# Decay attention and a squared-ReLU layer pair on one core: visits spaced apart, one product moved into a shared bank, and every engine's order planned anew

## The chip, the core and the metric

The kernel runs on one core of a Trainium2 chip, as one launch. The metric is the device time of that launch in microseconds (us), from three runs of the same program. One execution was also recorded by the hardware profiler. The engines are named as in the profile: PE (TensorE, the matrix engine; PEld are its weight loads), DVE (VectorE), ACT (ScalarE), POOL (GpSimd) and SP (SyncE, which here only issues transfers).

## The reference

```python
def _attn_ref(q, k, v, lam):                 # B=4, H=8, S=768, D=64, blocks of 64
    ...
    Dmask = np.where(rel >= 0, lam[:, None, None] ** rel[None, :, :], 0.0)
    ...
    for b in range(nb):
        ...
        intra = np.einsum('bhij,bhjd->bhid', np.einsum('bhic,bhjc->bhij', qb, kb) * Dmask[None], vb)
        inter = np.einsum('bhid,bhde->bhie', qb * lam_pow[None], kv_state)
        out[:, :, sl] = intra + inter
        kv_state = lam_block[...] * kv_state + np.einsum('bhsd,bhse->bhde', kb * rev_pow[None], vb)

def _moe_ref(x, w_in, w_out):                # x: 3072 tokens x 512, w_in: 512 x 2048, w_out: 2048 x 512
    h = np.maximum(x @ w_in, 0.0)
    return (h * h @ w_out).astype(np.float32)
```

The attention's output, with its heads side by side, is the input x of the two layers. Everything is 32-bit floating point, and the kernel keeps nearly that accuracy: each operand of a large product is split into a rounded part ("hi") and a remainder ("lo"), and three of the four partial products are summed.

## The kernel before, in words

**Chunks.** The 3072 tokens are 24 chunks of 128 tokens. Chunks 0 to 3 are the first of each batch; they are computed whole at the front, one after the other (scores of the chunk, sums for its state, its result). The other 20 go in pairs, in *visits*: one visit finishes the old pair (its results, in two halves: state products, `bank<-s,qv` and `bank<-qv,hold` in the trace) and opens the new one (its scores, `bank<-qv,ka`). All are small multiplications (64x64). The table `VISITS` says before which step a visit's first and second part stand: the result halves in one, the rest in the other. Between them the values of a chunk have to be scaled by powers of the decay, either by eight ScalarE multiplications of 128x64 (L564) or by one VectorE multiplication of 128x512 (L567); `weighted` chooses by the chunk's number. `dot` copies (L736) on ScalarE tie the two halves of a result together: PE's next half waits for them.

**Layers.** Four chunks make a tile of 512 tokens. For tiles 0 and 1 the first layer is 32 *steps* (`first_layer`, L770), one for each tile and each block of 128 hidden columns, of 12 multiplications 128x512; the results go through ReLU and square on ScalarE (L781, L782), and those not kept go to one of two buffers `sp` and from there to memory (spilled, L785). For the very first two blocks a step is cut in halves of 256 columns, so that the first half can go ahead of chunks 2 and 3. The other 16 chunks go in two passes (p = 0, 1) of four tiles as a scheme of seven products for a 2x2 block multiplication: `first_products` makes 8 groups of 7 products (each six multiplications 128x512, 1.36 us), `second_products` makes 56 products for the second layer. Within a group, products 1, 6 and 7 accumulate in bank "x", 2 in "y", 5 and 3 in "v", 4 in "z"; ScalarE copies the running sum of "x" to buffers `u` (r1, r2, r3; L893), so that product 6 waits for copy r1 and 7 for r2; VectorE adds bank and copy (L897), and ScalarE applies ReLU and square (L898, L899). The passes stand in this order: steps with visits; first products of p = 0; second products of p = 0; second products of tiles 0 and 1 (called p = 2), with five more visits between them (`INSIDE`); first and second products of p = 1.

**Weights.** Differences of weight blocks are made by VectorE (L820 to L826), split by ScalarE and VectorE (L804, L805), written to memory (`kept<-pw`) and read back by each product (`b<-kept`, L862) into few buffers `b`: four for the first 16 reads. A second-layer product takes its hidden block from ScalarE's cast and VectorE's remainder (L943, L944), which are let go three products ahead.

**Order.** No engine's order stands in the source. Each operation is entered with its dependences, its buffers and a modelled cost; `Plan.order` then sets the order of each engine by modelled time and a number for each operation, the long table `DUE`. The program is written out in that order, so each engine works its own list strictly in turn, and SP's list is the order in which all transfers are issued. The constants `FETCH`, `FETCH_LATER` and `FETCH_END` are the planner's cost of a refill of PE's program code, and up to which modelled time which of them holds. The code itself comes by a queue of its own, "q8 instruction" in the profile.

## Time and profile before

| | us |
|---|---|
| time, median of 3 runs (lowest, highest) | 557.48 (554.11, 558.42) |
| the profiled execution's own time | 559.53 |
| its span, first to last instruction | 557.8 |
| PE busy | 542.3 (97%) |
| DVE busy | 448.5 (80%) |
| ACT busy | 355.4 (64%) |
| mean busy share of the 16 DMA engines, whole span | about 0.8 |
| mean granted clock of TensorE | 0.993 of full |

PE is at work nearly all the time. So the table is read from its rest: 557.8 less 542.3 leaves 15.5 us without a matrix multiplication, and a mean clock below 1 says that some of the busy time ran slow. Where both lie is what the waits and the timeline of PE tell.

### The profile page before, as it was taken

The page shows a single profiled execution, that of the slowest core. Times are in us where ns is not written, and L with a number is a line of the kernel's source. Part 1 is how long each engine was busy: PE and PEld are TensorE (multiplying, and loading weights), DVE is VectorE, ACT ScalarE, POOL GpSimd, SP SyncE. Part 2 cuts the span into 40 slices and gives each one's busy share as a digit, 9 for nine tenths or more (in the row PEclk, how much of TensorE's full clock was granted, in tenths as well). Part 3 has the DMA queues.
Part 4 walks back from the last instruction along what each step waited for, and adds up shares of the span by engine and source line. Part 5 has one row for each costly group of instructions (what it writes and reads, how often), then busy time and mean ns, then how long its engine had stood idle before and what let it go on. Part 6 is the DMA issues. An engine that isn't in the chain of part 4 may idle for free.

```text
span 557.8 us, 12919 instructions
## 1 busy us (share of the span) xinstructions
PE 542.3 (97%) x4822; PEld 446.6 (80%) x4822; DVE 448.5 (80%) x897; ACT 355.4 (64%) x758; POOL 5.1 (1%) x10
## 2 busy tenths in 40 slices
PE   8898999998999999889999999999999999999997
PEld 7786787886888888768888888888888888888885
DVE  4999798998999999969967779999923334579864
ACT  4699677885799989844544333456456667655441
POOL 3000000000000000000000000000000000000000
PEclk9999899998999999999999999999999999999999
DMA  8978799989999867889999999447876776777763
GB/s 300 333 257 307 259 331 316 334 273 345 337 330 349 317 227 264 274 302 317 342 335 337 352 335 315 136 132 191 240 255 195 194 193 194 195 189 214 210 184 113
DMA packets 73406, 148.19 MB, mean 266 GB/s; under 512 B 7936, under 2 KB 14848, under 8 KB 73344
## 3 DMA queue, kind: packets, MB, share of 16 engines
q1 hardware_dynamic: 73056, 147.22, 80.2%
q8 instruction: 38, 0.62, 0.4%
q14 instruction: 24, 0.20, 0.1%
q10 hardware_dynamic: 288, 0.14, 0.1%
HBM read 106.18 MB, written 41.16 MB: 264 GB/s over the span
## 4 chain that ended last, share of the span: by engine, by line
PE 55%; DVE 6%; DMA 3%; issue 1%; ACT 0%; DVEq 0%; SPq 0%
PE bank L517 55%; DMA b<-kept 2%; DVE h L897 2%; DVE v L944 1%; DVE pw L805 1%; DVE part L805 1%; DMA kept<-part 0%; DVE m L494 0%; DVE m L826 0%; DMA kept<-pw 0%; DVE rs L826 0%; DVE m L496 0%; DVE h L951 0%; DVE m L492 0%; DVE rs L820 0%
## 5 line engine op out<-in xcount | busy, mean ns | idle before, releaser
L517 PE MATMUL bank<-v,b 128*128 128x512 f32 x1008 | 232.9, 391 | 3.1 <-ACT pw L804 1.5
L517 PEld LDWEIGHTS bank<-v,b 128*128 128x128 f32 x1008 | 188.1, 188 | 44.3 <-issue 3.0
L943 ACT CAST v<-h 128x512 fp32r<-128x512 f32 x168 | 101.8, 622 | 100.4 <-PE bank L517 73.4
L944 DVE TENSOR_TENSOR v<-h,v 128x512 fp32r<-128x512 f32 x168 | 113.5, 689 | 33.5 <-ACT v L943 29.8
L770 PE MATMUL bank<-xs,wi 128*128 128x512 f32 (+1 forms) x408 | 94.6, 388 | 4.3 <-issue 2.2
L770 PEld LDWEIGHTS bank<-xs,wi 128*128 128x128 f32 x408 | 74.2, 192 | 20.1 <-issue 2.5
L897 DVE TENSOR_TENSOR h<-bank,u 128x512 f32<-128x512 f32 x64 | 43.9, 691 | 46.1 <-ACT u L893 32.1
L951 DVE TENSOR_TENSOR h<-h,h 128x512 f32<-128x512 f32 x96 | 63.7, 689 | 0.8 <-DMA h<-spill 0.3
L898 ACT ACTIVATE h<-h 128x512 f32<-128x512 f32 x64 | 39.8, 628 | 13.4 <-DVE h L897 12.9
L899 ACT ACTIVATE h<-h 128x512 f32<-128x512 f32 x64 | 39.9, 630 | 0.7
L893 ACT COPY u<-bank 128x512 f32<-128x512 f32 x48 | 27.8, 580 | 14.9 <-PE bank L517 14.5
L564 ACT ACTIVATE qv<-qv,small 128x64 f32<-128x64 f32 x123 | 32.0, 339 | 3.8 <-POOL small L438 3.5
L517 PE MATMUL bank<-qv,ka 64*64 64x64 f32 (+2 forms) x1344 | 31.2, 224 | 0.7 <-issue 0.3
L517 PEld LDWEIGHTS bank<-qv,ka 64*64 64x64 f32 (+2 forms) x1344 | 27.8, 139 | 3.7 <-issue 2.2
L804 ACT CAST pw<-m 128x256 fp32r<-128x256 f32 x56 | 21.5, 403 | 9.3 <-DVE m L826 4.9
L805 DVE TENSOR_TENSOR pw<-m,pw 128x256 fp32r<-128x256 f32 x56 | 22.9, 423 | 3.2 <-ACT pw L804 3.0
L517 PE MATMUL bank<-sum_s,b 128*128 128x512 f32 x96 | 24.5, 391 | 0.0
L490 ACT ACTIVATE m<-st 128x512 f32<-128x512 f32 x32 | 21.2, 675 | 4.7 <-DMA st<-w 4.7
L517 PE MATMUL bank<-sum_a,b 128*128 128x512 f32 x96 | 24.2, 389 | 0.0
L517 PE MATMUL bank<-sum_a,wi 128*128 128x512 f32 x96 | 24.2, 389 | 0.0
L517 PEld LDWEIGHTS bank<-s,qv 64*64 64x64 f32 (+1 forms) x704 | 16.0, 137 | 9.2 <-issue 4.6
L517 PE MATMUL bank<-sum_t,part 128*128 128x512 f32 x96 | 23.1, 389 | 0.0
(83 smaller groups left out, 632.4 us busy)
## 6 DMA issues: line engine op xcount, KB each, us to landing
b<-kept SPq DMA_DIRECT2D x224, 256.0 KB, 3.1
st<-w SPq DMA_DIRECT2D x32, 512.0 KB, 4.9
kept<-pw SPq DMA_DIRECT2D x56, 256.0 KB, 3.6
ka<-ka SPq DMA_DIRECT2D x23, 512.0 KB, 5.8
qv<-qv SPq DMA_DIRECT2D x23, 512.0 KB, 6.1
kept<-part SPq DMA_DIRECT2D x32, 256.0 KB, 3.0
kept<-wi SPq DMA_DIRECT2D x24, 256.0 KB, 3.8
out<-end SPq DMA_DIRECT2D x23, 256.0 KB, 3.6
```

The costliest lines, as they stand in the source:

```text
L517: nc.tensor.matmul(*args, **kw, skip_group_check=True)
L564: self.o_vd = [plan.op("ACT", act(D) + 0.11, key, lambda i=i: nc.scalar.mul(v()[:, i], v()[:, i], wdec[:, i:i + 1]), [self.o_qv[1], o_pow] ...
L770: nc.tensor.matmul(at(h)[:, cs], wt[:, cc, :], xt[:, cc, cs], start=k == 0, stop=k == 3 * NCC - 1)
L804: oh = plan.op("ACT", act(256), key, lambda: nc.scalar.copy(at(part)[:, 0], side(k)), deps, raws + [part])
L805: ol = plan.op("DVE", tt(256), key, lambda: nc.vector.tensor_tensor(out=at(part)[:, 1], in0=side(k), in1=at(part)[:, 0], op=ALU.subtract), ...
L893: return plan.op("ACT", act(WIDE) - 0.03, key - 6, lambda: nc.scalar.copy(at(dst), at(banks[k])), [o], [banks[k], dst])
L897: o = plan.op("DVE", tt(WIDE), key - 6, lambda: nc.vector.tensor_tensor(out=at(b), in0=at(banks[k]), in1=at(a), op=ALU.add), deps, [banks[ ...
L898: o1 = plan.op("ACT", act(WIDE) + 0.01, key, lambda: nc.scalar.activation(at(b), at(b), AF.Relu), [o], [b])
L899: o1 = plan.op("ACT", act(WIDE) + 0.01, key, lambda: nc.scalar.activation(at(b), at(b), AF.Square), [o1], [b])
L943: oh = plan.op("ACT", act(WIDE) + 0.01, key - 16, lambda: nc.scalar.copy(rounded[hi.slot], at(b)), made[t, 2 * j + e], [b, hi], after)
L944: ol = plan.op("DVE", tt(WIDE), key - 16, lambda: nc.vector.tensor_tensor(out=rounded[lo.slot], in0=at(b), in1=rounded[hi.slot], op=ALU.su ...
L951: made[o] = [plan.op("DVE", tt(WIDE), when, lambda: nc.vector.tensor_tensor(out=at(h[o]), in0=at(h[a]), in1=at(h[b]), op=op), deps + made[ ...
```

## The change: spacing, a bank, a split and a new plan

What it does:

- `VISITS` moves the second part of the sixth visit from step 23 to step 25, and the last visit from step 27 to step 28. `INSIDE` moves three second parts by one or two products.
- `VS_END = 24`: the values of chunks 16 to 23 are scaled by eight ScalarE multiplications each instead of one VectorE multiplication.
- In `first_products` bank "z" is gone. Product 4 accumulates onto bank "x" after 1, 6 and 7, and waits for copy r3; its block is then ReLU straight from the bank (`squared` holds the square), so that one VectorE addition per group (16 in all) vanishes. Product 1 of the next group moves between 7 and 4.
- `FETCH`, `FETCH_LATER`, `FETCH_END` change, and `DUE` is all new; with it every engine's order. The DUE rows below stand for the whole table.

```diff
 DUE = [
-    0, 1, 2, 3, 2, 14, 5, 6, 5, 6, 8, 13, 18, 17, 7, 15, 9, 12, 14, 18, 29, 24, 13, 37, 32, 33, 36, 37, 41, 40, 16, 46, 43, 44, 46, 47, 54, 48, 10,
+    0, 1, 2, 3, 2, 18, 6, 17, 1, 0, 11, 17, 14, 20, 10, 28, 23, 8, 16, 31, 43, 35, 13, 35, 19, 12, 29, 34, 38, 41, 14, 46, 40, 21, 42, 39, 57, 49, 16,
...
-FETCH, FETCH_LATER, FETCH_END = 4.5, 3.2, 40.0
+FETCH, FETCH_LATER, FETCH_END = 4.75, 3.3, 260.0
...
-HALVED, HALF_KEY = 2, 3.0
+HALVED, HALF_KEY, VS_END = 2, 3.0, 24
...
-VISITS = [(3, 3), (6, 7), (10, 11), (14, 15), (18, 19), (22, 23), (27, 27)]
-INSIDE = [(1, 4, 4), (1, 11, 14), (1, 19, 22), (1, 27, 30), (1, 36, 36)]
+VISITS = [(3, 3), (6, 7), (10, 11), (14, 15), (18, 19), (22, 25), (28, 28)]
+INSIDE = [(2, 4, 4), (2, 11, 16), (2, 19, 23), (2, 26, 30), (2, 36, 36)]
 FIRST_ORDER = [1, 2, 6, 5, 7, 4, 3]
-AT_ONCE = [1, 2, 4, 6, 5, 7, 3]
+AT_ONCE = [1, 2, 6, 5, 7, 4, 3]
...
-            split = (VS if self.i else VS_FIRST) if self.i < N_ALONE else VS_LATER if self.i < N_PLAIN + 8 else 0
+            split = (VS if self.i else VS_FIRST) if self.i < N_ALONE else VS_LATER if self.i < VS_END else 0
...
-        banks, r, h, made = {k: Buf("bank") for k in "xyvz"}, [Buf("u" if p or j else "u0") for _ in range(3)], hidden[p], ready_h[p]
-        where = {1: "x", 2: "y", 6: "x", 5: "v", 7: "x", 4: "z", 3: "v"}
+        banks, r, h, made = {k: Buf("bank") for k in "xyv"}, [Buf("u" if p or j else "u0") for _ in range(3)], hidden[p], ready_h[p]
+        where = {1: "x", 2: "y", 6: "x", 5: "v", 7: "x", 4: "x", 3: "v"}
...
-                x, first = sums[g][:, :, k:k + 2], i in (1, 2, 5, 4)
+                x, first = sums[g][:, :, k:k + 2], i in (1, 2, 5)
...
+        def squared(t, f, o):
+            b = h[t, f]
+            made[t, f] = [plan.op("ACT", act(WIDE) + 0.01, key, lambda: nc.scalar.activation(at(b), at(b), AF.Square), [o], [b])]
...
             if i == 4:
-                st["p4"] = product(4)
-            if "r3" in st and "p4" in st:
-                block("z", 1, f0, r[2], [st.pop("p4"), st["r3"]])
+                b, o = h[1, f0], product(4, [st["r3"]])
+                squared(1, f0, plan.op("ACT", act(WIDE) - 0.02, key - 6, lambda: nc.scalar.activation(at(b), at(banks["x"]), AF.Relu), [o], [banks["x"], b]))
...
             k = order.index((j, 1))
-            order[k - 1], order[k] = order[k], order[k - 1]
+            order.insert(k - 2, order.pop(k))
...
-            if (j, i) == order[-1]:
+            if (j, i) == order[-2]:
                 product(LAST_ORDER[0], 0, twice[p])
```

Lines after the table stand one or two higher in the new program (L517 is L518 there, L781 is L782).

PE at the end of the front, before: chunk 3's sums (`64x64 x8`), its result (`bank<-s,qv`, eight rows of which the first two are shown), and then the second halves of the steps of blocks 0 and 1. `wi_66` and `wi_67` are the weights of those blocks.

```order
L517 MATMUL bank_65<-qv_3_89,ka_3_85 128x128
L770 MATMUL bank_59<-xs_220,wi_67 128x256 x12
L517 MATMUL bank_60<-qv_3_89,ka_3_85 64x64 x8
L517 MATMUL bank_58<-s_3_133,qv_3_89 64x128
L517 MATMUL bank_58<-s_2_132,qv_3_89 64x128
...
L770 MATMUL bank_61<-xs_220,wi_66 128x256 x12
L770 MATMUL bank_59<-xs_220,wi_67 128x256 x12
L770 MATMUL bank_62<-xs_220,wi_68 128x512 x12
```

The same place in the changed program (`table` rows are filler multiplications, whose result nobody reads):

```order
L518 MATMUL bank_65<-qv_3_89,ka_3_85 128x128
...
L518 MATMUL bank_59<-qv_3_89,ka_3_85 64x64 x8
L443 MATMUL bank_63<-table_219 128x128
L518 MATMUL bank_63<-s_3_133,qv_3_89 64x128
L518 MATMUL bank_63<-s_2_132,qv_3_89 64x128
...
L771 MATMUL bank_60<-xs_220,wi_67 128x256 x12
L771 MATMUL bank_61<-xs_220,wi_66 128x256 x12
L771 MATMUL bank_60<-xs_220,wi_67 128x256 x12
L771 MATMUL bank_58<-xs_220,wi_68 128x512 x12
```

The first half of block 1's step (`wi_67`) moved from ahead of chunk 3's sums to behind its result.

ACT around the last visit's `dot` copies, before: `sp` blocks are ReLU and square of a step, `pw` casts belong to weight differences, `m<-st` begins the conversion of a loaded weight block, `sum_a<-xk` belongs to the new pair's operands.

```order
L781 ACTIVATE sp_168<-bank_62 128x512
L782 ACTIVATE sp_168<-sp_168 128x512
L804 CAST pw_190<-m_162 128x256
L781 ACTIVATE sp_167<-bank_61 128x512
L736 COPY small<-bank_60 128x1
L490 ACTIVATE m_162<-st_206 128x512
L736 COPY small<-bank_63 128x1
L782 ACTIVATE sp_167<-sp_167 128x512
```

The same place in the changed program:

```order
L782 ACTIVATE sp_167<-bank_63 128x512
L805 CAST pw_190<-m_164 128x256
L783 ACTIVATE sp_167<-sp_167 128x512
L491 ACTIVATE m_162<-st_206 128x512
L491 ACTIVATE m_164<-st_205 128x512
L782 ACTIVATE sp_168<-bank_62 128x512
L737 COPY small<-bank_60 128x1
L783 ACTIVATE sp_168<-sp_168 128x512
L737 COPY small<-bank_64 128x1
```

A step's ReLU still stands directly ahead of the copies; the conversions of two weight blocks moved ahead of it, and no `pw` cast is left between the two.

PE in the first groups of pass 0, before (one row is one product; products 1, 2, 6, 5, 7, 4 of group 0 with 1 of group 1 behind 4, then 3; `sum_` names the token operand):

```order
L517 MATMUL bank_60<-sum_a,wi_66 128x512 x6
L517 MATMUL bank_59<-sum_a,wi_66 128x512 x6
L517 MATMUL bank_60<-sum_s,part_187 128x512 x6
L517 MATMUL bank_63<-sum_t,part_185 128x512 x6
L517 MATMUL bank_60<-sum_t,part_186 128x512 x6
L517 MATMUL bank_58<-sum_z,part_188 128x512 x6
L517 MATMUL bank_64<-sum_a,wi_68 128x512 x6
L517 MATMUL bank_63<-sum_s,wi_67 128x512 x6
```

The same place in the changed program:

```order
L518 MATMUL bank_59<-sum_a,wi_66 128x512 x6
L518 MATMUL bank_64<-sum_a,wi_66 128x512 x6
L518 MATMUL bank_59<-sum_s,part_187 128x512 x6
L518 MATMUL bank_61<-sum_t,part_185 128x512 x6
L518 MATMUL bank_59<-sum_t,part_186 128x512 x6
L518 MATMUL bank_58<-sum_a,wi_68 128x512 x6
L518 MATMUL bank_59<-sum_z,part_188 128x512 x6
L518 MATMUL bank_61<-sum_s,wi_67 128x512 x6
```

Product 4 (`sum_z`) now writes the bank of 1, 6 and 7, and one product stands between it and 7.

## Rows read from the trace of the kernel before

**Rows 1.** The page: PE's busy time, and PE's code queue (packets, MB, share).

```profile
PE 542.3 (97%) x4822; PEld 446.6 (80%) x4822; DVE 448.5 (80%) x897; ACT 355.4 (64%) x758; POOL 5.1 (1%) x10
...
q8 instruction: 38, 0.62, 0.4%
```

**Rows 2.** Waits of PE: line, releaser, us in total, times, longest.

```profile
PE bank L770 <- issue: 2.2, 1, 2.2
PE bank L517 <- ACT small L736: 2.1, 1, 2.1
PE bank L770 <- ACT xs L632: 1.9, 1, 1.9
PE bank L517 <- ACT pw L804: 1.5, 1, 1.5
...
PE bank L517 <- DMA b<-kept: 1.0, 2, 0.7
PE bank L517 <- ACT v L943: 0.5, 1, 0.5
PE bank L517 <- issue: 0.3, 1, 0.3
PE bank L517 <- ACT qv L564: 0.3, 1, 0.3
```

**Rows 3.** Stretches: length, busy PE, PEld, DVE, ACT, POOL, clock, DMA share, GB/s.

```profile
55.20:58.70 3.50, 3.50 (x10) 2.74 (x9) 3.50 (x10) 0.82 (x2) 0.00 (x0) 0.51 0.97 335
...
133.70:137.20 3.50, 3.50 (x68) 3.02 (x65) 3.24 (x10) 2.81 (x8) 0.00 (x0) 0.51 0.98 312
50.00:52.41 2.41, 2.40 (x129) 2.01 (x128) 2.14 (x5) 2.37 (x6) 0.00 (x0) 1.00 1.03 394
```

**Rows 4.** PE's timeline at the front's end: start, length, group, idle before.

```profile
23.20 1.68 PE L770 MATMUL bank<-xs,wi 128*128 128x256 f32 x12
```

**Rows 5.** VectorE's timeline in the same stretch.

```profile
26.88 0.69 DVE L700 TENSOR_TENSOR xr<-bank,rdec 128x512 f32<-128x512 f32 x1
```

**Rows 6.** PE's timeline around the visit before the eighth step.

```profile
51.90 0.51 PE L770 MATMUL bank<-xs,wi 128*128 128x512 f32 x1
54.62 7.58 PE L770 MATMUL bank<-xs,wi 128*128 128x512 f32 x25 [2.21 <-issue]
```

**Rows 7.** ScalarE at the last visit of the first part.

```profile
132.74 0.60 ACT L781 ACTIVATE sp<-bank 128x512 f32<-128x512 f32 x1 [0.26 <-DMA spill<-sp]
133.24 0.15 ACT L736 COPY small<-bank 128x1 f32<-128x1 f32 x1
```

**Rows 8.** Stretches of the same view as rows 3: first products, then later ones.

```profile
140.00:194.00 54.00, 54.00 (x240) 44.71 (x239) 53.05 (x123) 47.92 (x105) 0.00 (x0) 1.00 0.97 338
194.00:234.00 40.00, 39.25 (x174) 32.14 (x172) 40.00 (x90) 37.05 (x78) 0.00 (x0) 1.00 0.70 239
234.00:256.00 22.00, 19.67 (x82) 15.07 (x83) 16.70 (x30) 10.20 (x18) 0.00 (x0) 1.00 0.93 319
256.00:400.00 144.00, 144.00 (x1549) 119.37 (x1548) 128.15 (x237) 67.95 (x127) 0.00 (x0) 1.00 0.83 275
```

**Rows 9.** Groups by line: busy us, mean ns, idle before and releasers.

```profile
L897 DVE TENSOR_TENSOR h<-bank,u 128x512 f32<-128x512 f32 x64 | 43.9, 691 | 46.1 <-ACT u L893 32.1 <-PE bank L517 13.3
...
L564 ACT ACTIVATE qv<-qv,small 128x64 f32<-128x64 f32 x123 | 32.0, 339 | 3.8 <-POOL small L438 3.5 <-DMA qv<-qv 0.2
L893 ACT COPY u<-bank 128x512 f32<-128x512 f32 x48 | 27.8, 580 | 14.9 <-PE bank L517 14.5
...
L567 DVE TENSOR_TENSOR qv<-qv,small 128x512 f32<-128x512 f32 x8 | 5.5, 687 | 0.0
```

**Rows 10.** Transfers of the page: KB each, median us from issue to landing.

```profile
qv<-qv SPq DMA_DIRECT2D x23, 512.0 KB, 6.1
```

**Rows 11.** The page's groups of casts and remainders for second-layer products.

```profile
L943 ACT CAST v<-h 128x512 fp32r<-128x512 f32 x168 | 101.8, 622 | 100.4 <-PE bank L517 73.4
L944 DVE TENSOR_TENSOR v<-h,v 128x512 fp32r<-128x512 f32 x168 | 113.5, 689 | 33.5 <-ACT v L943 29.8
```

More of the change, by code (lines that the diff above doesn't have):

```diff
@@ L1039 @@
     twice = [first + 56 * A_PROD]
-    twice = [twice[0], 0, twice[0] + 56 * A_PROD]
+    twice = [twice[0], 0, twice[0] + 56 * A_PROD + STRETCH * 2 * sum(not p for p, _, _ in INSIDE)]
     third = twice[2] + 56 * A_PROD + STRETCH * 8
@@ L1049, in visit_at @@
         p, a, c = INSIDE[v - len(VISITS)]
-        return twice[2] + A_PROD * a + STRETCH * sum(x <= a for _, x, _ in INSIDE) * 2
+        return twice[p] + A_PROD * a + STRETCH * 2 * sum(x <= a and q == p for q, x, _ in INSIDE)
     chunks = []
@@ L1116, in firsts @@
             k = order.index((j, 1))
-            order[k - 1], order[k] = order[k], order[k - 1]
+            order.insert(k - 2, order.pop(k))
         for j, i in order:
-            if (j, i) == order[-1]:
+            if (j, i) == order[-2]:
                 product(LAST_ORDER[0], 0, twice[p])
             runs[j](i)
-            if j == NF // 2 - 1 and i in (2, 6, 3):
+            if j == NF // 2 - 1 and i in (2, 7, 4):
                 gate[p].append(end[0])
@@ L1128, in seconds @@
             for j in range(NF // 2):
-                for v, (_, a, c) in enumerate(INSIDE):
-                    if p == 2 and n == a:
+                for v, (q, a, c) in enumerate(INSIDE):
+                    if (p, n) == (q, a):
                         one, two = visiting(len(VISITS) + v)
@@ L1134, in seconds @@
                             rest[c] = two
-                if p == 2 and n in rest:
+                if p != 1 and n in rest:
                     linked(rest.pop(n))
```

4 lines of the change are left out of this document (1 added, 3 removed), and 167 rows, old and new, of the table DUE.

## The prediction, as it stood before the run

> **What bounds the kernel now.** I read the page first, for which engine is at work all the time: PE, with 542.3 us of the span, while the rest idle far more [rows 1]. Then PE's waits, because 15.5 us is all that PE leaves, and they come in a few pieces [rows 2]: one wait for "issue" (2.2, called B here), one for the dot copies of L736 (2.1, C), one for the cast L632 (1.9, A), and three behind one another in the second products of pass 0 (1.5, 1.0 for two, 0.5: together 3.0, D). Two of 0.3 follow; the start and the end hold most of the rest and are not touched by the change. Then the granted clock by stretches: right after B and right after C it is 0.51, for about 3.5 us each [rows 3], that is the lower of the two levels (1.2 instead of 2.4 GHz). Each costs 3.5 × 0.49 = 1.7 us more. After the waits of 1.9 and 1.5 no stretch shows it. So the most that a better order can return is A 1.9, B 2.2 + 1.7, C 2.1 + 1.7, D 3.0 and 0.6: 13.2 us. Elsewhere PE runs through: 54 of 54 us and 144 of 144 [rows 8], at 1.36 us a product. The number of products is the same after the change, so work that other engines are spared counts only where it ends one of these waits.
>
> **The sum by parts.** The profiled execution took 559.53 us; I make the sum against that, and then go to the median of the three runs, 557.48, which is 2.05 lower.
>
> *A, end of the front.* Chunk 3's result has to go through an addition on VectorE (L700, 0.69) and a cast on ScalarE before the step of block 0 can go on, and the addition began at 26.88, behind other work of a VectorE that has no gap there [rows 5]. PE waits 1.9. The new order puts the first half of block 1's step, which needs only chunks 0 and 1, into that place; such a half takes 1.68 us [rows 4]. In its old place between two pieces of chunk 3 it would be missed only if chunk 3's scores then hold PE up, and there the new plan has filler and half of block 0's step. Cover alone returns 1.68. VectorE has also less between the last operands, since conversions of weight blocks stand later. I take the whole wait, 1.9. Bounds: 0.3, if the wait reappears ahead of chunk 3's result for want of that half; 2.8, if the chunk's loads, which the new order of transfers puts ahead of one 512 KB weight load each, also pull the chain forward by some 0.9.
>
> *B, the wait for issue.* PE's program came in 38 blocks of 0.62 MB together; 4822 multiplications and 4822 loads in 38 blocks are 254 instructions each [rows 1]. A first-layer step needs 24 instructions for 2.72 us, so that a block lasts some 29 us; but the visit before the eighth step has 129 multiplications and 128 loads, a whole block, in 2.41 us, with the DMA engines full [rows 3]. PE stops one multiplication of the step further, for 2.2 us [rows 6]: I read this as the next block still on its way. The new plan leaves out one filler multiplication and, counting the instructions of both programs, the block ends four rows later, after two more multiplications of that step, 0.2 us each. If the block arrives when it did, the wait is 2.2 − 0.45 = 1.75. That is between the 1.5 and 1.9 that left the clock at full and away from the 2.1 and 2.2 that didn't, so I take it that the slow stretch goes too: 0.45 + 1.7 = 2.1. Bounds: −0.3 (block a little later, clock falls) and 3.9 (all of it).
>
> The Trainium skill speaks against this term: "Runtime: NRT & Kernel Launch", section "Instruction fetch mechanics", says that code is prefetched in order and that crossing a 16 KiB boundary costs little, mostly hidden. The row of 2.2 us differs at one crossing of 38, and agrees for nearly all others. By that rule B would have another cause, its term would be 0, and the sum below 2.1 smaller (the second rival).
>
> *Small waits.* The 0.3 for issue has the same cause, in the visit at step 23; its second part now stands at 25, two steps of 2.72 us more between the parts. The 0.3 for L564 is a visit's scaling that comes late. Both go: 0.6, bounds 0 and 0.6.
>
> *C, the last visit.* ScalarE does its list in order. Just ahead of the dot copy at 133.24 stands the ReLU of a step, which waits for a spill of one of the two `sp` buffers and ends its 0.60 us only then [rows 7]; PE waits for the copy, 2.1. In the new order a step's ReLU still stands directly ahead, but the visit stands one step later in the program and the step before it is not the one that has just handed over a buffer, and no `pw` cast stands between. I reckon with 1.0 left, which is the copy's own way plus the one ReLU that PE cannot avoid (0.60 [rows 7]) and its wait, and with no fall of the clock: 1.1 + 1.7 = 2.8. Bounds: −0.5 (same wait with a weight block's conversion, which waits for its load, in the list ahead) and 3.8.
>
> *D, the reads of weight differences.* PE waits here for operands of which the last to come are reads `b<-kept` [rows 2], in a stretch with the DMA engines at 0.93 [rows 8]. The transfers of that stretch are the same in kind and number in the new list. VectorE is better off: it is busy 40.00 of 40.00 us up to 234 [rows 8], and eight additions fewer in pass 0 are 8 × 691 ns = 5.5 us [rows 9]. But what PE waits for last is the transfer, and SP issues it when a buffer comes free, not when VectorE is done. Term 0; bounds −1.5 and 2.5, the latter if stores of differences leave earlier and clear the queue.
>
> *Product 4 in the shared bank.* 16 additions on VectorE go (8 × 0.69 a pass). In exchange product 4 waits for copy r3. One product, 1.36 us, now stands between 7 and 4; the copy takes 0.58 [rows 9], so it has 0.7 us to spare. Before, the same copies r1 and r2 stood under 6 and 7 in the same way, and PE lost nothing by them from 140 to 194 [rows 8]. The copies themselves mostly wait for PE (14.5 us idle before them, 48 of them [rows 9]), so ScalarE is there in time, except where it is full (37 of 40 us from 194 to 234 [rows 8]). If a copy comes 0.9 late there, product 4 loses 0.2. Term −0.4; bounds 0 and −1.0. Pass 1's groups are free: PE is all that is busy there.
>
> *Values on ScalarE.* Eight VectorE multiplications (5.5 us) become 64 of 339 ns each (21.7 us) [rows 9]. ScalarE has 68 of 144 us in the stretch where they fall [rows 8], and no addition or cast waits there that isn't covered by the three products that casts run ahead, so 0. What it costs without that cover is the third rival.
>
> *Give-back.* From 140 to 194 the DMA engines are at 0.97 and VectorE at 53 of 54 [rows 8]. If PE arrives there 6 us earlier, less slack is left, and a part may come back as waits of products for differences or for hidden blocks. VectorE's own saving by then is about that of the additions passed so far. I take −1.0; bounds 0 and −3.
>
> Sum: 1.9 + 2.1 + 0.6 + 2.8 + 0 − 0.4 + 0 − 1.0 = 6.0. Profiled execution: 559.5 − 6.0 = 553.5; on the median's scale 557.5 − 6.0 = **551.5 us**.
>
> **Rivals.**
>
> 1. *D goes as well.* If VectorE's 5.5 us bring the stores forward, the reads at 230 to 251 find a freer queue: up to 2.5 more, and with B and A at their upper bounds some 2 more. For it: the stretch before it moves only 0.70 of what the DMA engines can [rows 8], so there is room for earlier stores. Against: SP's list is in order. Time: about 548 (546 to 549.5).
>
> 2. *The clock still falls, or B is not what I take it for.* If both remaining waits are followed by a slow stretch, 3.4 comes back: 555. If B stays whole, 2.1 comes back, 553.6; with a give-back of 3, as PE runs into a VectorE and a DMA that are full from 140 on, 556 to 557. For it: the two waits differ by only some tenths from those with a clock fall. The change then does little that can be measured.
>
> 3. *Slower: ScalarE held by a late chunk.* The 64 new multiplications stand in ScalarE's list, and the first of each eight waits for its chunk, 512 KB, 6.1 us median from issue to landing [rows 10]. Before, VectorE took that wait. Behind them in the list stand the casts for coming second-layer products. A cast may begin three products ahead, 4.08 us; cast and remainder take 0.62 + 0.69 [rows 11], so some 2.7 us are to spare. It decides from where the load lands more than 2.7 us after ScalarE has reached the multiplication. Each of the eight chunks then stops PE for the excess; eight times 1.5 us is 12, which ends the gain and makes 551.5 + 12 = 563.5. With a wait of more than 2 us, the clock might fall too. Against it: the new list puts three to four products and visit parts between issue and multiplication, about the load's median, so a wait of 0 to 2 us is likelier, which is covered.
>
> **How the numbers follow.** A measurement of this kernel can tell about 1% from no change, 5.6 us, so 551.9 and 563.1 are the marks. Forecast (550 to 553.5) 0.40, a little over half of it below 551.9; rival 1 0.24; rival 2 and the give-back (553.5 to 559) 0.25; rival 3, or another new wait of its size, 0.11. Faster by over 1%: 0.23 + 0.24 = 0.47. Slower by over 1%: of the last case, and a little for costs that nobody priced, 0.11. Within 1%: 0.42. The range leaves out the lower end of rival 1 and rival 3: 546 to 558.5; its upper end is the sum with the bounds of B, C and the give-back taken together (−0.3, 0.5, −3 instead of 2.1, 2.8, −1: 558).
>
> **What would show it.** A: no wait of L771's matmuls for L633, and block 0's second half beginning before 28. B: the wait for issue between 1.4 and 2.0 us, clock 1.00 in the stretch behind it. C: the wait for L737 about 1, clock full behind it. Small: no wait in the visit at step 23 or 25. D: waits of about 3 us for `b<-kept` at the same products. Product 4: L898 (before L897) 48 times instead of 64, PE whole from 140 to 194. Values: L565 187 times instead of 123, and no wait of PE for L944 in 256 to 400. What would make it wrong: waits of PE of over a microsecond where there are none now, above all in the second products of p = 2, or a new long wait for issue, since the code's blocks end elsewhere in all later visits.

## The result, and the profile after

The changed kernel takes 551.58 us (median of 11 runs, 550.62 to 553.66), the kernel before on the same chip 557.79 (11 runs, 553.69 to 559.69): a ratio of 0.9905, with an interval of 0.9878 to 0.9931. That is 6.2 us less; 6.0 were forecast. The profiled execution took 553.66 us with a span of 551.9, 5.9 less than before, and is the longest of the eleven, as the profiled one of before was near its longest. So the two can be set beside each other, and the question is whether the 5.9 are made of the terms that were forecast. They are only partly, and the profiled execution is not the usual one.

The page's first line of engines, to be read against [rows 1]:

```profile
PE 540.5 (98%) x4820; PEld 446.2 (81%) x4820; DVE 434.6 (79%) x873; ACT 370.2 (67%) x822; POOL 5.1 (1%) x10
```

VectorE has 24 instructions and 14 us less, ScalarE 64 instructions and 15 us more, as the two edits say. The waits of PE after, to be read against [rows 2]:

```profile
PE bank L518 <- DMA b<-kept: 2.6, 2, 2.0
PE bank L518 <- ACT small L737: 2.1, 1, 2.1
PE bank L443 <- DVE table L427: 1.5, 1, 1.5
PE bank L771 <- DVE xs L634: 0.7, 1, 0.7
PE bank L771 <- issue: 0.4, 1, 0.4
PE bank L518 <- issue: 0.2, 1, 0.2
```

A has gone from 1.9 to 0.7, B from 2.2 to 0.4, both small waits are gone and one of 0.2 is new, at another visit (81 us); C is what it was, 2.1, and D is 2.6 instead of 3.0. What each stretch gained is read best from windows cut at the same instruction in both kernels, so that each holds the same work (the counts of PE are the same but for missing records). The cuts are the first multiplications of the third first-layer step (the first whole one) and of the ninth, the first product of pass 0, the 57th and the 78th, and PE's last. Before:

```profile
31.64:58.84 27.20, 24.98 (x459) 20.32 (x458) 26.85 (x61) 21.79 (x56) 0.00 (x0) 0.94 0.86 295
58.84:150.09 91.25, 88.49 (x1409) 72.98 (x1408) 81.39 (x194) 69.20 (x183) 0.00 (x0) 0.98 0.90 311
150.09:226.29 76.20, 76.20 (x337) 63.06 (x336) 75.90 (x175) 70.16 (x152) 0.00 (x0) 1.00 0.84 292
226.29:259.28 32.99, 29.91 (x127) 23.21 (x126) 27.69 (x50) 18.14 (x35) 0.00 (x0) 1.00 0.94 322
259.28:554.10 294.82, 294.78 (x2211) 243.53 (x2209) 212.27 (x369) 155.85 (x278) 0.00 (x0) 1.00 0.76 233
```

After (columns as in [rows 3]: length, busy PE, PEld, DVE, ACT, POOL, clock, DMA share, GB/s):

```profile
29.48:53.28 23.80, 23.42 (x458) 19.08 (x457) 23.77 (x53) 21.07 (x55) 0.00 (x0) 1.00 0.85 293
53.28:143.67 90.39, 88.08 (x1409) 72.82 (x1408) 85.55 (x204) 70.42 (x185) 0.00 (x0) 0.98 0.95 329
143.67:219.95 76.28, 76.28 (x338) 62.94 (x336) 76.05 (x175) 69.29 (x153) 0.00 (x0) 1.00 0.85 298
219.95:253.50 33.55, 30.92 (x127) 24.52 (x126) 23.98 (x44) 22.22 (x51) 0.00 (x0) 0.95 0.92 309
253.50:548.20 294.70, 294.66 (x2211) 243.72 (x2209) 203.60 (x354) 167.60 (x325) 0.00 (x0) 1.00 0.76 233
```

The lengths give the account: the front 31.64 − 29.48 = 2.16; the stretch with B 27.20 − 23.80 = 3.40; the rest of the first layer with the small waits and C 0.86; the first products −0.08; the second products with D −0.56; all the rest 0.12. Together 5.90. Where the slow stretches of the clock are now:

```profile
51.20:54.70 3.50, 3.50 (x16) 2.84 (x17) 3.50 (x9) 1.80 (x3) 0.00 (x0) 1.00 0.85 241
130.00:133.40 3.40, 3.40 (x67) 3.06 (x68) 3.04 (x9) 1.75 (x5) 0.00 (x0) 0.51 0.90 318
229.00:232.30 3.30, 3.30 (x8) 2.61 (x9) 0.94 (x3) 1.34 (x5) 0.00 (x0) 0.50 0.70 271
```

The one behind B is gone, the one behind C is still there, and D, whose wait of 2.0 is now in one piece, has got one. Of the eleven executions five have a mean clock of 1.000 (spans of 549.2 to 549.9 us) and four one of 0.999; the profiled one, with two falls, is at 0.994. A typical execution of the changed kernel is some 2 us shorter than the profiled one, and has fewer falls or none. Of the 58 executions of the kernel before that were taken beside the experiments, 55 have a mean clock of 0.998 or less; their median is 0.9965, that of the eleven 0.999. A slow stretch of 3.5 us at half clock takes 0.003 off the mean. So by the medians about one stretch, 1.7 us of the 6.2, is the clock's (an estimate from these numbers), while the profiled pair has two slow stretches on either side.

### The profile page after: what moved, and what is told of

It reads as the page before. It is cut to its first block, busy times and chain, and to the rows that moved or that the text cites. A ratio compares the mean times of both kernels' runs of the same rounds, so it can differ in the third digit from the quotient of the medians.

```text
span 551.9 us, 12964 instructions
## 1 busy us (share of the span) xinstructions
PE 540.5 (98%) x4820; PEld 446.2 (81%) x4820; DVE 434.6 (79%) x873; ACT 370.2 (67%) x822; POOL 5.1 (1%) x10
## 4 chain that ended last, share of the span: by engine, by line
PE 68%; DVE 16%; DMA 8%; ACT 4%; issue 3%; SPq 1%; DVEq 0%; ACTq 0%
PE bank L518 62%; PE bank L771 5%; DMA b<-kept 3%; DMA spill<-sp 2%; DVE pw L806 2%; DVE m L495 1%; DMA st<-w 1%; DVE rs L821 1%; DVE rs L827 1%; DVE m L497 1%; DMA kept<-pw 1%; DVE m L492 1%; DVE m L493 1%; DVE h L898 1%; DVE part L806 1%
## 5 line engine op out<-in xcount | busy, mean ns | idle before, releaser
L518 PE MATMUL bank<-v,b 128*128 128x512 f32 x1008 | 233.9, 392 | 2.6 <-DMA b<-kept 2.6
L518 PEld LDWEIGHTS bank<-v,b 128*128 128x128 f32 x1008 | 189.5, 189 | 43.6 <-ACT v L945 3.4
L771 PE MATMUL bank<-xs,wi 128*128 128x512 f32 (+1 forms) x408 | 93.0, 384 | 1.2 <-DVE xs L634 0.7
L771 PEld LDWEIGHTS bank<-xs,wi 128*128 128x128 f32 x408 | 72.9, 189 | 16.8 <-issue 1.0
L898 DVE TENSOR_TENSOR h<-bank,u 128x512 f32<-128x512 f32 x48 | 33.1, 691 | 50.2 <-ACT u L894 28.0
L565 ACT ACTIVATE qv<-qv,small 128x64 f32<-128x64 f32 x187 | 49.7, 338 | 6.5 <-POOL small L439 3.4
L904 ACT ACTIVATE h<-h 128x512 f32<-128x512 f32 x64 | 39.6, 633 | 0.8
L899 ACT ACTIVATE h<-h 128x512 f32<-128x512 f32 x48 | 30.2, 633 | 7.6 <-DVE h L898 7.0
L518 PE MATMUL bank<-qv,ka 64*64 64x64 f32 (+2 forms) x1344 | 30.3, 224 | 0.0
L518 PEld LDWEIGHTS bank<-qv,ka 64*64 64x64 f32 (+2 forms) x1344 | 27.5, 139 | 2.2 <-issue 1.5
L518 PE MATMUL bank<-sum_s,b 128*128 128x512 f32 x96 | 24.4, 389 | 0.0
L518 PE MATMUL bank<-sum_a,wi 128*128 128x512 f32 x96 | 24.2, 389 | 0.0
L518 PE MATMUL bank<-sum_a,b 128*128 128x512 f32 x96 | 24.2, 389 | 0.0
L518 PEld LDWEIGHTS bank<-s,qv 64*64 64x64 f32 (+1 forms) x704 | 16.2, 138 | 9.4 <-issue 3.5
L518 PE MATMUL bank<-sum_t,part 128*128 128x512 f32 x96 | 23.1, 390 | 0.0
L518 PE MATMUL bank<-sum_t,b 128*128 128x512 f32 x96 | 23.1, 389 | 0.0
```

The costliest lines, as they stand in the source:

```text
L518: nc.tensor.matmul(*args, **kw, skip_group_check=True)
L565: self.o_vd = [plan.op("ACT", act(D) + 0.11, key, lambda i=i: nc.scalar.mul(v()[:, i], v()[:, i], wdec[:, i:i + 1]), [self.o_qv[1], o_pow] ...
L771: nc.tensor.matmul(at(h)[:, cs], wt[:, cc, :], xt[:, cc, cs], start=k == 0, stop=k == 3 * NCC - 1)
L898: o = plan.op("DVE", tt(WIDE), key - 6, lambda: nc.vector.tensor_tensor(out=at(b), in0=at(banks[k]), in1=at(a), op=ALU.add), deps, [banks[ ...
L899: squared(t, f, plan.op("ACT", act(WIDE) + 0.01, key, lambda: nc.scalar.activation(at(b), at(b), AF.Relu), [o], [b]))
L904: made[t, f] = [plan.op("ACT", act(WIDE) + 0.01, key, lambda: nc.scalar.activation(at(b), at(b), AF.Square), [o], [b])]
```

## The experiments

Orders were changed behind the planner: `move(o, j)` takes one operation out of the finished list and puts it at place j, where nothing in between shares a buffer with it or depends on it. All other operations keep their order. e6 and e9 change operations and keep the lists; e10 and e11 are planned anew. Ratios are to the kernel before, on the same chip in the same hour; the changed kernel's is 0.9905.

| run | median us (runs) | ratio to before, interval |
|---|---|---|
| e1_relu_behind | 551.28 (10) | 0.9911, 0.9881 to 0.9941 |
| e2_all_behind | 552.24 (8) | 0.9917, 0.9888 to 0.9945 |
| e3_loads_later | 553.76 (10) | 0.9937, 0.9900 to 0.9975 |
| e4_half_moved | 556.24 (1) | one run |
| e5_no_spacing | 577.74 (1) | one run |
| e6_dve_back | 560.60 (4) | 1.0085, 1.0052 to 1.0118 |
| e7_rows | 551.88 (1) | one run |
| e8_ka_later | 553.58 (1) | one run |
| e9_values_dve | 553.82 (10) | 0.9953, 0.9926 to 0.9979 |
| e10_own_bank | 555.44 (10) | 0.9965, 0.9942 to 0.9989 |
| e11_visits_close | 553.90 (6) | 0.9944, 0.9918 to 0.9969 |
| e12_both | 552.47 (10) | 0.9930, 0.9898 to 0.9962 |

### What C waits for: ReLU behind the dot copies, then the conversions too

```diff
+    move(square, rank(last_) + 1)      # last_: the last dot copy on ScalarE at the last visit
+    move(relu, rank(last_) + 1)
```

> The changed kernel with one edit: at the last visit of the first part, ReLU and square of a step stand behind the four dot copies in ScalarE's list instead of ahead of and between them. Theory (in-order list): PE's wait of 2.12 us there is what stands ahead of the copy, of which the ReLU is 0.60 and its own wait for a spill 0.56; two conversions of weight blocks still stand ahead. The wait falls to 0.9 to 1.2 us, no slow stretch of the clock follows it, and the profiled span falls from 551.9 by 1.0 to 2.8. Rival (the copy waits for its product, or for transfers whatever the order): the wait stays at 1.9 us or more and the time does not move.

In the changed kernel ScalarE's timeline shows the same picture as [rows 7], the ReLU that waits for a spill directly ahead of the copy:

```profile
129.18 0.60 ACT L782 ACTIVATE sp<-bank 128x512 f32<-128x512 f32 x1 [0.56 <-DMA spill<-sp]
129.67 0.15 ACT L737 COPY small<-bank 128x1 f32<-128x1 f32 x1
```

With the ReLU behind the copies PE's wait for ScalarE's copy is 0.3 instead of 2.1, but 1.0 for the other chunk's copies, which are on VectorE, takes its place. The waits of e1 for those copies:

```profile
PE bank L522 <- DVE small L742: 1.0, 1, 1.0
...
PE bank L522 <- ACT small L742: 0.3, 1, 0.3
```

In sum 1.3, within a tenth of what was expected, though for another reason; the clock stays full, and the span is 548.8. The median says something else: 0.9911 is not below 0.9905.

Other runs tell why. In e3 to e9 the lists of ScalarE and VectorE up to 140 us are the changed kernel's, so C is untouched there. PE's waits for the copies at that visit are 1.3 (e3), 0.7 (e4), 1.3 (e5), 1.1 (e6), 0.95 (e7), 0.8 (e8) and 0.6 (e9) in sum, and behind none of them is a slow stretch. The waits of e3 and of e9:

```profile
129.32 0.47 PE L522 MATMUL bank<-s,qv 64*64 64x64 f32 x14 [1.31 <-ACT small L742]
```

```profile
129.39 0.39 PE L518 MATMUL bank<-s,qv 64*64 64x64 f32 x10 [0.58 <-DVE small L738]
```

The stretch from the ninth step to the first product, 91.25 us before and 90.39 in the profiled execution of the changed kernel, is 87.1 to 88.9 in six of these seven and 90.1 in e8. That of e7 and of e9:

```profile
54.14:141.82 87.68, 86.39 (x1410) 71.33 (x1408) 84.63 (x202) 70.50 (x185) 0.00 (x0) 1.00 0.97 336
```

```profile
53.39:141.72 88.33, 86.84 (x1409) 71.61 (x1408) 85.40 (x204) 70.19 (x186) 0.00 (x0) 1.00 0.96 337
```

In e1 it is 88.9. So the profiled execution, with its 2.12 and the slow stretch, is the exception, and e1 removed next to nothing of what the changed kernel usually waits. In e5, e6, e7 and e9 the ReLU ahead of the copy did not wait for a spill; in e3 it waited 0.65, and PE 1.3.

```diff
+    ahead = relu                        # chains: the two conversions L491 and what follows them on VectorE
+    for o in reversed(chains):
+        move(o, rank(ahead))
+        ahead = o
```

> As the run with the ReLU behind the copies, and the two conversions of weight blocks (with the VectorE operations that follow them up to there) behind the copies too. Theory (in-order list): nothing is ahead of the copy, PE's wait is 0 to 0.3 us, the profiled span 1.9 to 3.8 below 551.9. Rival (the time is only moved): VectorE and the transfers are full from here to the first products, so that the conversions, one to two us later, come back as waits of PE behind 132 us; the sum of PE's waits up to the second products falls by less than half of 2.1.

There is no wait for a copy any more. But PE now waits at the second group of first products, which had no wait in either kernel. The waits of e2 that are new:

```profile
PE bank L522 <- ACT v L950: 2.0, 2, 1.5
...
PE bank L522 <- ACT u L899: 1.3, 1, 1.3
...
PE bank L522 <- DVE sum_t L844: 0.4, 1, 0.4
```

1.3 + 0.4 of the 2.1 came back at 144 and 147 us, where VectorE and the transfers are full, and the sum of PE's waits up to the second products is 5.1 instead of 4.9. The rival "moved" is right in this execution: the wait ahead of the full stretch cost little to have. That the full engines catch up in such a wait is how I read it; it is not shown.

### What D waits for: loads of chunks out of the way of the reads

```diff
+    for k, n in ((16, 15), (17, 19)):   # reads: SP's reads of weight differences, in order
+        for i, o in reversed(list(enumerate(sorted(tags[f"scale{k}"], key=rank)))):
+            move(o, rank(reads[n + 6 + i]) + 1)
+        for o in reversed(tags[f"load{k}"]):
+            move(o, rank(reads[n]) + 1)
```

> The changed kernel with four loads of 512 KB (chunks 16 and 17) and their scaling moved some ten reads of weight differences later in SP's and ScalarE's lists; the chunks are needed only some 60 us later. Theory (transfers bound the reads): a read issued at 223.0 stands behind some 1.5 MB and takes 5.7 us; without the loads ahead of it about 3.5. The waits of 1.96 and 0.67 us for these reads fall below 0.5 in sum, no slow stretch follows, and the profiled span falls by 2 to 4.3. Rival (the stores of differences or VectorE's work for them bound the reads): both waits stay within 0.3 of what they are. Second rival (moved): waits of the same size appear at the reads behind the new place.

The two waits for reads, 2.0 and 0.7, fell to one of 1.0; but a new one of 2.2 stands some ten products later. Waits of PE in e3, and what ScalarE did there:

```profile
PE bank L522 <- ACT qv L570: 2.2, 1, 2.2
...
PE bank L522 <- DMA b<-kept: 1.0, 1, 1.0
```

```profile
242.35 0.35 ACT L570 ACTIVATE qv<-qv,small 128x64 f32<-128x64 f32 x1 [1.71 <-DMA qv<-qv]
242.60 0.60 ACT L950 CAST v<-h 128x512 fp32r<-128x512 f32 x1
```

This is the prediction's third rival, made by hand: the load was issued at 236.96, its scaling stood six reads behind, ScalarE came to it 1.71 us too early and held the cast of a product behind it. In the changed kernel the planner leaves enough room, and no such wait is there. e12 then puts the scaling ten reads further, and has e1's edit too:

```diff
-            move(o, rank(reads[n + 6 + i]) + 1)
+            move(o, rank(reads[n + 16 + 2 * i]) + 1)
```

> The changed kernel with the ReLU behind the dot copies, and with the loads of chunks 16 and 17 ten reads later as before in these runs, but their scaling sixteen and more reads behind the loads instead of six. Theory (ScalarE was held by the late chunk): the wait of 2.19 us for the scaling is gone, the waits for reads sum to 0.5 to 1.5, the wait for the dot copies to about 1.3; profiled span 547 to 548.5 and time 549 to 550.3, below the changed kernel's 551.6. Rival (the waits move): a wait of over 1.5 us at other reads or visits, time 551 and more.

The wait for the scaling is gone, and the wait for the reads is back at a later read:

```profile
PE bank L522 <- DMA b<-kept: 2.3, 1, 2.3
...
PE bank L522 <- ACT v L950: 0.9, 1, 0.9
```

0.9930 is no better than the changed kernel. D's waits sum to 2.6 in the changed kernel, 3.2 in e3 and 3.2 in e12: the place moves, the sum does not fall. From the 57th to the 78th product PE takes 33.6 us in the changed kernel, 32.6 in e3, 33.8 in e12, and 31.9 to 35.1 in the runs that leave the order there alone (e1, e4 and e7 to e9), so two runs could not show a small gain. From 216 to 252 us the DMA engines are busy for 0.86 of the time in the changed kernel and for 0.89 and 0.81 in e3 and e12. I had read D as the sum of what has to be moved there; with 0.81 that is not shown, and what bounds D stays open.

### What A is worth: the half step behind instead of in the gap

```diff
+    half_ = [o for o in done if o.eng == "PE" and any(b.kind == "run" for b in o.bufs)]
+    move(half_[1], rank(half_[2]) + 1)
```

> The changed kernel with the first half of block 1's step moved from behind chunk 3's result to behind the second half of block 0's step. Theory (the half covers the chain over VectorE and ScalarE): the wait behind chunk 3's result grows from 0.75 us by the half's length, 1.7, to 2.2 to 2.7, about as before the change with the filler gone, and PE reaches the later steps 1.5 to 1.9 us later. Rival (the chain itself came earlier by the new order of loads and VectorE's work, and the half covers little): the wait stays below 1.5.

The waits of e4 behind chunk 3's result:

```profile
PE bank L776 <- ACT xs L638: 1.7, 1, 1.7
...
PE bank L776 <- DVE xs L639: 0.7, 1, 0.7
```

2.4 in sum instead of 0.7: the half covers its own length, 1.7, as the prediction has it. That execution also has a slow stretch behind the wait and one at D. PE reached the third step at 32.5 us, where it does so at 29.4 to 29.8 in all other runs and at 31.6 in the kernel before.

### What B waits for: four instructions more at the front

```diff
+        for _ in range(2):
+            nc.tensor.matmul(tiles["bank"][bank_][:, 0:1], zero[:, 0:P], zero[:, 0:1], start=True, stop=True)
```

> The changed kernel with two more tiny filler multiplications at the front, four instructions more, so that every block of PE's code ends four instructions earlier in the program, as before the change. Theory (a block must be there when PE crosses its end): in the visit before the eighth step PE has 0.45 us less work until the block's end, and the wait for issue there grows from 0.38 (0.4 in two runs of the changed order, none in two others) to 0.8 or 0.9; in the two waits of a few tenths at other visits it moves by less than 0.1. Rival (the arrival of the block depends on the loads alone and varies more than that): no wait of over 0.5 at that place.

PE's timeline of the changed kernel there, and then of e7:

```profile
49.73 0.97 PE L771 MATMUL bank<-xs,wi 128*128 128x512 f32 x3
51.08 1.21 PE L771 MATMUL bank<-xs,wi 128*128 128x512 f32 x4 [0.38 <-issue]
```

```profile
48.73 1.11 PE L522 MATMUL bank<-qv,ka 64*64 64x64 f32 x63
51.05 0.27 PE L522 MATMUL bank<-qv,ka 64*64 64x64 f32 x1 [1.22 <-issue]
```

In the trace the two fillers are four multiplications and four loads (4824 of each instead of 4820), and PE stops just four multiplications earlier: the last of the visit and three of the step. It goes on at the same moment, 51.05 and 51.08. The wait grew by 0.84, about the work that now lies behind the stop (three times 0.23 and one of the visit's). The length alone would not show this, since without fillers it was 0.9 in e6 and 1.2 in e4, at the changed kernel's place. But the place of the stop moved by just what was put in ahead: PE waits at a fixed place in its code, as the prediction said of the block. When the awaited thing comes varies: PE goes on 3.4 us after the visit's first multiplication in the changed kernel, 3.9 in e6 and 4.2 in e4. My expectation of 0.45 had counted four instructions; eight it is. The rest of this execution was shorter by other things, so that its time is no measure of it.

```diff
+    move(ka_, rank(st_) + 1)            # a 512 KB chunk load behind a 512 KB weight load
```

> The changed kernel with one 512 KB load of a chunk moved behind one 512 KB load of weights in SP's list, near 45 us, so that less is under way when PE asks for the code block of the visit before the eighth step. Theory (the code block queues behind the loads): PE's wait for issue of 0.38 us goes, and the block's request to its arrival is shorter by about 1 us. Rival (only the place of the block's end counts): the wait stays at 0.3 to 0.5.

There is no wait for issue there in e8. But e1, e3, e11 and e12, whose orders up to there are the changed kernel's or nearly, have none either, while e10 has 0.2, e2 and e9 have 0.4 and e6 has 0.9. So the wait varies by as much between executions, and this run tells nothing. Where it is 0, a wait of 0.3 to 0.7 for VectorE (L607, L602 in e11) stands at the next visit.

### What the two edits off PE are worth

```diff
+            move(tags[f"p1_{p}_{j + 1}"][0], rank(tags[f"p4_{p}_{j}"][0]) + 1)
```

> The changed kernel with product 1 of the next group moved back from ahead of product 4 to behind it, 7 times in each pass, so that 4 follows 7 directly. Theory (one product covers the copy r3): product 4 waits for the copy each time, 0.58 us and the way there and back, 0.7 to 1.0 us, 14 times: the span grows by 10 to 14 us to 562 to 566, and where ScalarE is late by more. Rival (copies run well ahead of need, or the wait overlaps with what PE waits for anyway): under 4 us in sum.

The waits of e5 for the copies:

```profile
PE bank L522 <- ACT u L899: 17.0, 21, 1.9
```

577.74 us: without the product between 7 and 4 the bank edit would cost over 20 us. That is more than expected: 14 of the 21 waits stand at product 4, as expected, and seven more at product 7 (`sum_t`), where the copy comes late too. In pass 1 each wait at product 4 is 0.68. It shows what cover the one product gives; in the changed kernel there is no wait for a copy at all.

```diff
-                squared(1, f0, plan.op("ACT", ..., lambda: nc.scalar.activation(at(b), at(banks["x"]), AF.Relu), ...))
+                squared(1, f0, plan.op("ACT", ..., lambda: (nc.scalar.activation(at(b), at(banks["x"]), AF.Relu),
+                    nc.vector.tensor_tensor(out=at(b), in0=at(b), in1=at(b), op=ALU.max)), ...))
```

> The changed kernel with VectorE's load put back: one operation 128x512 that changes nothing in each of the 16 blocks from bank x, and the values of chunks 16 to 23 scaled by one VectorE multiplication instead of eight on ScalarE; 24 times 0.69 is 16.5 us more on VectorE, 16 to 21 less on ScalarE. Orders and banks as in the changed kernel. Theory (VectorE's relief is not what paid): PE's waits up to the first products are as they are, those of the second products of pass 0 grow by 0 to 1 us, the time by less than 1.5. Rival (the relief of a full VectorE pays): waits for VectorE of 2 us and more in sum between 140 and 260 us, and the time grows by 3 or more.

My theory, that VectorE's relief is not what paid, fell: 560.6 us, above the kernel before. The waits of e6:

```profile
PE bank L518 <- ACT u L895: 3.7, 6, 0.8
...
PE bank L518 <- DVE s L603: 1.0, 1, 1.0
```

It is too harsh, though, since VectorE's operation now stands between ScalarE's ReLU and square and so stops ScalarE's list. e9 and e10 therefore undo one edit each, in the form that the kernel before had it.

```diff
-        banks = {k: Buf("bank") for k in "xyv"}
+        banks = {k: Buf("bank") for k in "xyvz"}
...
-                b, o = h[1, f0], product(4, [st["r3"]])
+                b, p4 = h[1, f0], product(4)
+                o = plan.op("DVE", tt(WIDE), key - 6, lambda: nc.vector.tensor_tensor(out=at(b), in0=at(banks["z"]), in1=at(r[2]), op=ALU.add), [p4, st["r3"]], [banks["z"], b, r[2]])
```

> The changed kernel with product 4 back in a bank of its own and the 16 VectorE additions of its blocks back, PE's order as in the changed kernel, the other orders planned with the same numbers (an added operation stands right behind the addition of product 3's partner). It undoes the bank edit alone. Prediction's theory (the addition that vanishes is off the path): PE's waits from the first product to the 56th under 0.5 us in sum, time 551 to 553. Theory after the run with VectorE's load back (a VectorE that is full there holds ScalarE's list and with it the copies): waits for copies of 2 us and more in sum between product 14 and 56, later waits for reads as before the change, time 554 to 559.

Two stretches of e10 (columns as before), and two of its waits:

```profile
140.00:194.00 54.00, 54.00 (x240) 44.72 (x239) 53.85 (x125) 47.01 (x101) 0.00 (x0) 1.00 0.97 338
194.00:226.00 32.00, 30.32 (x130) 23.76 (x129) 32.00 (x72) 29.63 (x65) 0.00 (x0) 1.00 0.56 201
```

```profile
PE bank L518 <- ACT part L805: 0.5, 1, 0.5
PE bank L518 <- DVE part L806: 0.4, 1, 0.4
```

VectorE is at 32.00 of 32 us there, as it was before the change, and PE loses 1.7 us, 0.9 of it for weight differences (`part`) that come late. In the changed kernel the same window has PE at 32.00 and VectorE at 31.54. The time is 0.9965 of the kernel before, by the ratios 3.3 us more than the changed kernel, and the intervals do not meet. From the first product to the 57th e10 takes 79.0 us; e11 (below), which keeps the bank edit but was planned anew as e10 was, takes 77.6; the runs that leave the work ahead and the order there alone (e1, e3, e4, e7 to e9, e12) take 76.2 to 76.4. The stretch in e10, then in e11:

```profile
144.28:223.30 79.02, 77.34 (x337) 62.68 (x336) 78.87 (x180) 70.69 (x153) 0.00 (x0) 1.00 0.82 287
```

```profile
143.10:220.70 77.60, 77.08 (x337) 62.84 (x336) 75.67 (x174) 70.55 (x156) 0.00 (x0) 1.00 0.81 291
```

So a plan that does not fit costs 1.3 us there by itself, and of e10's 2.7 the bank edit's own share is not separated.

```diff
-    lambda i=i: nc.scalar.mul(v()[:, i], v()[:, i], wdec[:, i:i + 1])
+    lambda i=i: nc.scalar.mul(...) if self.i < N_PLAIN + 8 else nc.vector.tensor_tensor(out=v(), in0=v(), in1=..., op=ALU.mult) if i == H - 1 else None
```

> The changed kernel with the values of chunks 16 to 23 scaled by one VectorE multiplication each, in the place of the last of eight on ScalarE; all other orders as in the changed kernel. It undoes the split alone. Theory after the run with all of VectorE's load back (9 us slower): of its loss some 2.3 us lay between products 119 and 140, where only the values had moved, so the split pays about 2: waits of PE for VectorE or for code of 1 us and more in the visits of the second pass, time 553 to 555. Rival (the blocks in bank x were the whole loss): no wait of PE there, time 551 to 552.3.

Two of the waits of e9:

```profile
PE bank L518 <- issue: 1.5, 2, 0.8
...
PE bank L518 <- DVE s L603: 0.9, 1, 0.9
```

0.9953 is by the ratios 2.7 us more than the changed kernel, with intervals that just overlap. From the 78th product to PE's end e9 takes 296.9 us, 2.2 more than the changed kernel; the runs that change nothing there vary from 294.6 to 295.7. The wait for VectorE, late to a visit's masks (L603), stands at 346 us and also in e6, and in no kernel that has the edit; the kernel before, planned for VectorE's multiplication, has none there either. Of the two for issue one, 0.7, is at 318 us; waits of 0.3 to 1.0 stand there in e4, e7, e8 and e12 too, so it is not the edit's. What the edit itself pays in this plan is then about 1 us by the trace and up to 2.7 by the medians.

### The spacing of the visits

```diff
-VISITS = [(3, 3), (6, 7), (10, 11), (14, 15), (18, 19), (22, 25), (28, 28)]
+VISITS = [(3, 3), (6, 7), (10, 11), (14, 15), (18, 19), (22, 23), (27, 27)]
```

> The changed kernel with the visits of the first part where they were before (second part of the sixth at step 23, the last at 27), planned with the same numbers. It undoes the spacing alone. Theory (a block of code must come between two dense visit parts): a wait for issue of 0.3 us or more is back in the sixth visit's second part, and the last visit's wait for the dot copies is 1 to 2.5; time 0.3 to 2 us longer than the changed kernel, 551.9 to 553.6. Rival (the plan has to fit its visits): other orders shift, new waits of more than 1 us, time over 554. Second rival (no effect): 551 to 551.9.

The wait for issue in the sixth visit's second part is back with 0.2, less than the 0.3 expected; the last visit's is 0.7, no longer than in the runs that keep the spacing (0.6 to 1.3), where 1 to 2.5 was expected. Several of 0.3 to 1.0 stand elsewhere, of them

```profile
PE bank L518 <- ACT qv L565: 1.0, 1, 1.0
PE bank L518 <- issue: 0.8, 2, 0.5
```

Time 553.9, 0.9944: 2.2 us more than the changed kernel, intervals that overlap. Since the planner shifted other orders with it, this is a price of visits that the plan does not fit; what the spacing alone pays is not shown. `INSIDE`, in which the change moves two second parts (14 to 16, 22 to 23) and one first part (27 to 26), was left as changed.

## Why the prediction was right, and where its terms were not

The number was right to 0.1 us, and the sum of the profile to 0.1 us. That it is so close is luck. In the profiled pair C came 2.8 us short, and B, the bank and the give-back came out some 2.6 us better; in most of the other traced executions C came nearly as forecast. And executions of either kernel differ among themselves by 3 to 6 us.

*A*, forecast 1.9: 2.16 to the first step behind the front, 1.2 of it from the wait itself and the rest because PE reached the place earlier. Right in the main, and the cover of 1.7 is shown (e4). I had taken the whole wait; the 0.75 that is left is for VectorE's remainder (L634) instead of ScalarE's cast.

*B*, forecast 0.45 + 1.7 = 2.1: measured 3.40 with the clock. A stop at a fixed place in the code is right (e7), and the size was off, in the wait: 0.45 was reckoned from the place of the block's end with an arrival as before, but PE could also go on earlier, and 0.38 was left where I had set 1.4 to 2.0 as the sign. PE went on 4.75 us after the visit's first multiplication before (49.87 to 54.62) and 3.4 us after it now (47.70 to 51.08). In the new list of transfers one 512 KB load is issued in the 3 us ahead of the visit, where there were two (issued at 47.36 and 47.79); that these loads are the cause is argued and not shown (e8), and with one list of transfers the time varies from 3.4 to 4.2 (e6, e4), or there is no wait. There is only one trace of the kernel before, so how much of B is the order's is open.

The Trainium skill's rule that a crossing costs little, mostly hidden ("Runtime: NRT & Kernel Launch", section "Instruction fetch mechanics"), agrees with most crossings (38 blocks, and two waits for issue of 0.1 us or more before and two after), but not with this visit: PE waited 2.21 us there before, and 0.38 in the changed kernel and 1.22 in e7, where the stop moved with the code.

*C*, forecast 2.8: this step failed in the profiled execution and held in most others. I reckoned with a wait of 1.0 and no fall of the clock, because the step ahead of the visit should not be the one that has to wait for a spill. In the profiled execution it was: its ReLU waited 0.56 for the spill, two conversions stood ahead of it, and the wait was 2.12 again with the slow stretch behind it. The stretch from B to the first product gained 0.86 there, which is a little more than the 0.6 forecast for the small waits. In seven runs with the same lists the wait was 0.6 to 1.3 with no fall, and in six of them the stretch gained 2.3 to 4.2, where 2.8 + 0.6 were forecast. So the size was right for the usual execution; that it varies I had not reckoned with, and I had not counted what had come in ahead of the ReLU. In e2 nothing was left of the wait, and 1.7 reappeared 15 us later.

*D*, forecast 0: −0.56. The waits are shorter by 0.4, but 2.0 of them are in one piece with a slow stretch behind.

*Bank and give-back*, forecast −0.4 and −1.0: −0.08 together. Here a reason seems to have been missing. I took VectorE's relief for work off the path, worth nothing, and charged the give-back on the other side. PE did arrive 6 us earlier in a stretch in which VectorE has no time to spare, and nothing came back. That the relief is what kept it is likely and not shown: with the bank edit alone undone PE takes 79.0 us instead of 76.3 from the first product to the 57th (e10), but 1.3 of that a plan that does not fit costs too (e11). The values on ScalarE, forecast 0, paid 1 to 2.7 us further on (e9). These prices hold in a plan made for the edits. With e11's (2.2) and e4's (4.7 in one run) they sum to more than the whole gain, so they are no shares of it.

In the sum for the upper end of the range C stands with 0.5, though its own bound was −0.5; with that the end would have been 559.2 instead of 558.2.

The rivals: the first (D goes as well) did not come, and no order tried made it come. Of the second, the slow stretch behind C stayed in the profiled execution and a new one came behind D, but nine of the eleven executions have a mean clock of 0.999 or more; the give-back did not come. The third is possible, at 2.2 us for one chunk (e3) where 1.5 was named, but the plan avoids it.

## What to carry to other kernels

When an engine in front is made faster, ask which engines behind it are full, and whether they have been given the same amount of time; relief of a full engine that nobody waits for yet may be what makes the gain in front stay (e10 points to it). A wait of the bounding engine that ends just ahead of such a full stretch may come back when it is removed by itself, as in e2. Dense short instructions can use up a block of code before the next is there: here 257 in 2.41 us, where PE went on 3.4 to 4.8 us after the visit's start. A few instructions added far ahead move the place of the stop. And one trace is one execution: set the waits of several runs with the same order side by side before you call a step failed or right.

## What was not expected of the hardware

The length of a wait of PE does not tell whether the clock falls behind it. I had read from the kernel before that waits of up to 1.9 leave it at full. After the change the waits of 1.96 and 2.12 were followed by a slow stretch, as was 1.90 in e7; but 2.19 in e3, 1.86 in e1 and 2.43 in e10 were not. Nor has it to be one long wait: a slow stretch came behind 1.69 and 0.75 close together in e4, behind 1.54 and 0.59 in e10, and behind 1.08 and 1.08 in e12. The same program shows both: over the eleven executions of the changed kernel the mean clock is between 0.994 and 1.000, the span between 551.9 and 548.9.

The wait for issue at the visit before the eighth step, which I take for a wait for a block of code, varies between executions whose orders up to there are the same: none (e1, e3), 0.4 (the changed kernel, e2, e9), 0.9 (e6).
